# Linear attention and a convolved feed-forward block: query factors sent through memory, kv by heads, one PSUM store

## The chip, the cores and the metric

The kernel runs on one core of a Trainium2 chip. The engines are named as in the profile: PE is TensorE (its weight loads are listed as PEld), DVE is VectorE, ACT is ScalarE, POOL is GpSimd, and SP issues the DMAs. The metric is the device time of one execution in microseconds. A shorter time is better.

## What is computed

Four batches of four heads, 1088 positions, 32 columns a head. All arrays are float32 to the kernel; S1, S2 and the feed-forward weights arrive as float64 and are turned into float32 on the chip.

```
def phi(x):                       # r = 8
    a = einsum('rd,bhsd->bhsr', S1, x)
    b = einsum('rd,bhsd->bhsr', S2, x)
    return einsum('bhsi,bhsj->bhsij', a, b)   # 64 features per head
kv  = einsum('bhsf,bhsd->bhfd', phi(k), v)
z   = sum over s of phi(k)
x   = (phi(q) @ kv) / (phi(q) @ z + 1e-6)     # heads side by side: 128 columns
h   = max(x @ w_in, 0)                        # 128 -> 1024
c   = conv over the sequence, 3 taps, per feature
out = (h * sigmoid(c)) @ w_out                # 1024 -> 128
```

## The kernel before

The sequence of a batch is cut into 9 chunks of 128 positions, taken in 3 groups of 3 (`GC`, `NG`). The kernel has four parts.

*Keys, per batch and group.* `k_ab` (L518) projects a chunk by S1 and S2 at once; ACT copies the result out of PSUM (`k_take`, L522); `k_phi` forms the outer products with `outer` (L502) on DVE or POOL, as the table `kphi` says; `k_kv` (L556) multiplies them with v on two PE tiles of 128x64, each for two heads, so half of each result belongs to the wrong head and `k_kvmask` (L567) clears it. `k_kvt` transposes it and `k_kvtake` (L575) copies it. `k_z` (L536) multiplies the two key factors on one 32-column tile, `k_zmask` and `k_wz` (L544) turn that into 32 further columns of the query weights `wq`, so that the denominator comes out of the query projection.

*Queries, per batch and group.* `q_ab` (L583) projects, `q_take` (L587) copies, `q_ac`, `q_sum`, `q_rec`, `q_div` (L591 to L604) make the denominator and divide the first factor by it, `q_phi` forms the outer product (table `qphi`), `q_t` (L618) transposes it in six 128x128 pieces, `q_ttake` (L622) copies them, `q_x` (L628) multiplies by kv on two 128x64 tiles. `q_hi` (L642) and `q_lo` (L645) split x into two parts for the feed-forward products.

*Feed-forward.* The columns of all batches stand in one row and are cut into 9 segments of up to 510 columns (`SEGS`), times 8 blocks of features: 72 units. A unit runs `f_in` (three matmuls, L673 to L675), `f_relu` and `f_mid` on ACT (L680, L684), two taps on DVE (L688), `f_gate` on ACT (L694), `f_mul` on POOL (L699; the last unit on DVE) and `f_out` (L704), which accumulates over the 8 feature blocks. `f_store` (L710, L715) copies a segment and stores it.

*Weights.* `to_f32` (L428 to L465) converts the float64 words in pieces, with five passes on DVE, two on ACT and one on POOL.

The order of the work is planned in the program itself: `graph` lists each step with a cost and a key, `schedule` places them on four engines by those costs, and `in_order` (L731) issues them in that order, which then holds on each engine. Loads are issued first, in the order of the string `loads`, all from SP. Until 22 us of the plan, gaps on PE are filled with warming matmuls (L414). PSUM has eight banks: four for feed-forward units (`u`), one for the accumulation (`o`), three for everything else (`t`). All inputs have SBUF space of their own.

Of the kernel before, what the change touches and what calls it, by code (L numbers as in the profile page):

```python
# [31 lines left out]

GC = 3
NG = NCH // GC
GT = GC * P
NT = [min(GT, S - g * GT) for g in range(NG)]

# [9 lines left out]
C_ID = 0  # L47
C_KM = C_ID + P
C_ZM = C_KM + P
C_END = C_ZM + HR  # L50

W_S = 2 * HR
T_S2 = 0
T_CW = T_S2 + P
T_END = T_CW + NF * KT

# [3 lines left out]
LOADED = 512  # L60

CFG = {
    "loads": "s t k0 c v0 i0 q0 o0 o1 k1 i1 v2 k3 v1 q2 k2 v3 q1 q3",

    "F0": 16775.11,
    "P": 1995.06,
    "wlead": 1515.06,  # L70
    "outlag": 5.22,
    "tapa": 1050.8,
    "tkey": -31343.46,

    "kdue": [-105657.0, -48463.0, 35025.0, 47292.0],
    "kstep": [9195.0, 4315.0, -973.0, 12517.0],
    "kvlag": -871.37,

    "qlead": [[91584.0, 16163.0, 35465.0], [13701.0, 19977.0, 21211.0], [30185.0, 23965.0, 16558.0], [30572.0, 32036.0, 9517.0]],

    "kphi": ["DPP", "PPP", "PPP", "DPD"],
    "qphi": ["DPP", "DDD", "PPP", "PPP"],

    "late": 1,
    "fills": 22000.0,
}

POOLS = {"u": 4, "o": 1, "t": 3, "h": 6, "s": 3, "g": 6, "f": 3, "w": 3, "kab": 6, "kp": 4, "qs": 3, "qp": 2, "qt": 4, "kv": 2}
BEGIN = {"PE": 1100.0, "ACT": 3000.0, "DVE": 1800.0, "POOL": 1400.0}
KB = {"s": 64, "t": 156, "c": 147, "k": 557, "v": 590, "q": 557, "i": 524, "o": 524}  # L90
SEM = 45.0
FILL = 430.0

def c_pe(occ):
    return "PE", occ, occ + 170 + SEM, False


def c_act(n, ptr=0):  # L100
    return "ACT", 0.833 * n + 52 + 93 * ptr, 0.833 * n + 186 + 93 * ptr + SEM, False
# [10 lines left out]

def graph(cfg):
# [3 lines left out]
    landed = {}  # L117


    def ev(name, cost, deps, alloc=(), uses=(), key=0.0):  # L120
        for b, kind in alloc:
            kind_of[b] = kind
            users[b].append(name)
        for b in uses:
            users[b].append(name)
        events[name] = (cost, deps, [b for b, _ in alloc], key)

    issue, done = 730.0, 0.0
    for name in cfg["loads"].split():
        issue += 420  # L130
        done = max(issue + 1450, done) + KB[name[0]] / 0.345
        landed["dma", name] = done + 250

    for w, n, key in (("s", W_S, -5e4), ("t", T_END, cfg["tkey"])):
# [9 lines left out]
    ev("wqs", c_pool(B * W_S, 1.0), [("s", "value")], key=-4e4)  # L144

    f0, step = cfg["F0"], cfg["P"]
    for w in "io":
        for j in range(NCV):
            d, n = ("dma", f"{w}{j * CVT // LOADED}"), CVT
            key = f0 + (j * CVT // P + (0 if w == "i" else 3.2)) * step - cfg["wlead"]  # L150
            b, bf, bw = ("cv", w, j), ("f", w, j), ("w", w, j)
            ev((w, j, "e"), c_dve(n), [d], [(b, "t")], key=key)
            ev((w, j, "m"), c_dve(n), [d, (w, j, "e")], uses=[b], key=key)
            ev((w, j, "clamp"), c_dve(n), [(w, j, "e")], uses=[b], key=key)
            ev((w, j, "low"), c_act(n), [d], [(bf, "f")], key=key)
            ev((w, j, "f"), c_dve(n), [(w, j, "m"), (w, j, "low")], uses=[b, bf], key=key)
            ev((w, j, "power"), c_act(n), [(w, j, "clamp")], uses=[b], key=key)
            ev((w, j, "sign"), c_dve(n), [(w, j, "power")], [(bw, "w")], [b], key)
# [5 lines left out]
    def unit_of(b, g):  # L164
        c = 1 + b * PITCH + g * GT
        return next(s for s in range(NSEG) if OFF[s] + SEGS[s] + 2 > c) * NF

    def outer(name, where, deps, bank, alloc, uses, key):
        if where == "D":
            ev(name, c_dve(GC * H * RR), deps, [alloc], [bank, *uses], key)  # L170
        else:
            ev(name, c_pool(GC * H * RR, 1.745), deps, [alloc], uses, key)

    for b in range(B):
        due, ks, lag = cfg["kdue"][b], cfg["kstep"][b], cfg["kvlag"]
        for g in range(NG):
            key, t, kp, kv, ab = due + g * ks, ("kps", b, g), ("kp", b, g), ("kvps", b), ("kab", b, g)
            ev(("k_ab", b, g), c_pe(670), [("s", "value"), ("dma", f"k{b}")], [(t, "t")], key=key)
            ev(("k_take", b, g), c_act(192), [("k_ab", b, g)], [(ab, "kab")], [t], key)
            outer(("k_phi", b, g), cfg["kphi"][b][g], [("k_take", b, g)], t, (kp, "kp"), [ab], key)  # L180
            before = [("k_kv", b, g - 1)] if g else []
            ev(
                ("k_kv", b, g),
                c_pe(650),
                [("k_phi", b, g), ("dma", f"v{b}"), *before],
                [] if g else [(kv, "t")],
                [kv, kp] if g else [kp],
                key + lag,
            )
        key = due + 2 * ks  # L190
        abs_ = [("kab", b, g) for g in range(NG)]
        ev(("k_z", b), c_pe(580), [("k_take", b, g) for g in range(NG)], [(("zps", b), "t")], abs_, key)
        ev(("k_zmask", b), c_dve(32), [("k_z", b), ("dma", "c")], uses=[("zps", b)], key=key)
        ev(("k_wz", b), c_pe(270), [("k_zmask", b), ("t", "value")], [(("wzps", b), "t")], key=key)
        ev(("k_wq", b), c_act(32), [("k_wz", b)], uses=[("wzps", b)], key=key)
        key += lag
        ev(("k_kvmask", b), c_dve(128), [("k_kv", b, NG - 1), ("dma", "c")], uses=[("kvps", b)], key=key)
        ev(("k_kvt", b), c_pe(110), [("k_kvmask", b)], [(("kvtps", b), "t")], key=key)
        ev(("k_kvtake", b), c_act(128), [("k_kvt", b)], [(("kv", b), "kv")], [("kvtps", b)], key)
        for g in range(NG):  # L200
            key, q, x, qp = f0 + unit_of(b, g) * step - cfg["qlead"][b][g], ("qps", b, g), ("xps", b, g), ("qp", b, g)
            qs = ("qs", b, g)
            ev(("q_ab", b, g), c_pe(670), [("k_wq", b), "wqs", ("dma", f"q{b}")], [(q, "t")], key=key)
            ev(("q_take", b, g), c_act(192), [("q_ab", b, g)], [(qs, "qs")], [q], key)
            ev(("q_ac", b, g), c_dve(96), [("q_take", b, g)], uses=[q, qs], key=key)
            ev(("q_sum", b, g), c_dve(108), [("q_ac", b, g)], uses=[qs], key=key)
            ev(("q_rec", b, g), c_dve(72), [("q_sum", b, g)], uses=[qs], key=key)
            ev(("q_div", b, g), c_dve(96), [("q_rec", b, g)], uses=[q, qs], key=key)
            outer(("q_phi", b, g), cfg["qphi"][b][g], [("q_div", b, g)], q, (qp, "qp"), [qs], key)
            for pr in range(2):  # L210
                t, qt = ("qtps", b, g, pr), ("qt", b, g, pr)
                ev(("q_t", b, g, pr), c_pe(330), [("q_phi", b, g)], [(t, "t")], [qp], key)
                ev(("q_ttake", b, g, pr), c_act(384), [("q_t", b, g, pr)], [(qt, "qt")], [t], key)
            deps = [("q_ttake", b, g, 0), ("q_ttake", b, g, 1), ("k_kvtake", b)]
            uses = [("qt", b, g, 0), ("qt", b, g, 1), ("kv", b)]
            ev(("q_x", b, g), c_pe(700 * NT[g] / GT), deps, [(x, "t")], uses, key)
            ev(("q_hi", b, g), c_act(NT[g]), [("q_x", b, g)], uses=[x], key=key)
            ev(("q_lo", b, g), c_dve(NT[g]), [("q_hi", b, g)], uses=[x], key=key)

    for u in range(NU):  # L220
        s, f = divmod(u, NF)
        n, key = SEGS[s], f0 + u * step
# [96 lines left out]
def body(ctx: ExitStack, tc: tile.TileContext, qT, kT, v, pk, ps, pt, w_in, w_out, outT):  # L319
# [404 lines left out]
    for u in range(NU):  # L724
        ffn(u)
# [51 lines left out]
```

## Time and profile before

| what | value |
|---|---|
| time, median of 3 runs | 180.09 us (179.15 to 180.49) |
| span of the profiled execution, first to last instruction | 177.1 us |
| instructions | 2740 |
| granted TensorE clock, mean | 0.998 |
| read from memory, written | 9.28 MB, 2.23 MB |

No time of its own is given for the profiled execution beside its span; the median of the runs is 3.0 us above that span.

A group row of the profile names line, engine, operation, output and inputs by the program's names, shapes and count; then the total busy time, the mean of one instruction, and the idle time before it with what ended it. A row of the chain or the timeline begins with its start and its length in us. A row of a table of stretches gives the ends, the length, and the busy time of each engine with the number of instructions in brackets. In the slices of the span each digit is a busy share in tenths.

### The profile page before, as it was taken

The page shows a single profiled execution, that of the slowest core. Times are in us where ns is not written, and L with a number is a line of the kernel's source. Part 1 is how long each engine was busy: PE and PEld are TensorE (multiplying, and loading weights), DVE is VectorE, ACT ScalarE, POOL GpSimd, SP SyncE. Part 2 cuts the span into 40 slices and gives each one's busy share as a digit, 9 for nine tenths or more (in the row PEclk, how much of TensorE's full clock was granted, in tenths as well). Part 3 has the DMA queues.
Part 4 walks back from the last instruction along what each step waited for, and adds up shares of the span by engine and source line. Part 5 has one row for each costly group of instructions (what it writes and reads, how often), then busy time and mean ns, then how long its engine had stood idle before and what let it go on. Part 6 is the DMA issues. An engine that isn't in the chain of part 4 may idle for free.

```text
span 177.1 us, 2740 instructions
## 1 busy us (share of the span) xinstructions
PE 168.1 (95%) x872; PEld 109.2 (62%) x872; DVE 147.1 (83%) x288; ACT 145.6 (82%) x308; POOL 121.2 (68%) x116
## 2 busy tenths in 40 slices
PE   7997789998999999999999999999999999999992
PEld 6875567586766665755675655766455666566630
DVE  5259888969999786968897898899789999989981
ACT  4046558969997987998997989989999999999960
POOL 2065996686986446586766867689558699777670
PEclk9999999999999999999999999999999999999999
DMA  5999991000001000010000001000100100100101
GB/s 163 324 339 422 415 396 43 4 2 0 0 4 44 2 0 0 0 63 0 0 29 34 4 0 59 0 0 0 63 0 0 59 0 2 44 15 4 59 0 47
DMA packets 4477, 11.68 MB, mean 66 GB/s; under 512 B 496, under 2 KB 2416, under 8 KB 4464
## 3 DMA queue, kind: packets, MB, share of 16 engines
q1 hardware_dynamic: 4464, 11.51, 17.6%
q8 instruction: 7, 0.11, 0.3%
q14 instruction: 6, 0.05, 0.1%
HBM read 9.28 MB, written 2.23 MB: 65 GB/s over the span
## 4 chain that ended last, share of the span: by engine, by line
PE 83%; DVE 5%; POOL 4%; ACT 4%; issue 1%; POOLq 1%; ACTq 0%
PE o L704 33%; PE a L673 10%; PE a L674 8%; PE a L675 8%; PE t L556 5%; PE t L628 4%; PE t L618 4%; PE warm L414 4%; PE t L583 3%; POOL kp L502 3%; PE t L518 2%; POOL qp L502 1%; PE t L536 1%; ACT em L454 1%; ACT a L684 1%
## 5 line engine op out<-in xcount | busy, mean ns | idle before, releaser
L688 DVE SCALAR_TENSOR_TENSOR a<-h,pts,a 128x510 f32<-128x510 f32 (+2 forms) x144 | 102.6, 724 | 12.7 <-ACT a L684 9.9
L699 POOL TENSOR_TENSOR g<-h,s 128x510 f32<-128x510 f32 (+2 forms) x71 | 86.4, 1224 | 37.3 <-ACT s L694 30.3
L704 PE MATMUL o<-g,w_out_sb 128*128 128x510 f32 (+2 forms) x144 | 71.0, 579 | 0.4 <-POOL g L699 0.4
L684 ACT ACTIVATE a<-h,pts 128x510 f32<-128x510 f32 (+2 forms) x72 | 49.3, 686 | 0.9
L673 PE MATMUL a<-xhi,whi 128*128 128x512 f32 (+2 forms) x72 | 46.6, 648 | 0.9 <-ACT s L694 0.9
L680 ACT ACTIVATE h<-a 128x512 f32<-128x512 f32 (+2 forms) x72 | 42.2, 587 | 6.1 <-PE a L675 6.0
L694 ACT ACTIVATE s<-a 128x510 f32<-128x510 f32 (+2 forms) x72 | 41.9, 586 | 2.2 <-DVE a L688 1.8
L704 PEld LDWEIGHTS o<-g,w_out_sb 128*128 128x128 f32 x144 | 25.2, 189 | 10.7 <-POOL g L699 4.7
L674 PE MATMUL a<-xhi,wlo 128*128 128x512 f32 (+2 forms) x72 | 27.6, 384 | 0.0
L675 PE MATMUL a<-xlo,whi 128*128 128x512 f32 (+2 forms) x72 | 27.6, 383 | 0.0
L673 PEld LDWEIGHTS a<-xhi,whi 128*128 128x128 f32 x72 | 13.6, 189 | 15.2 <-issue 8.5
L674 PEld LDWEIGHTS a<-xhi,wlo 128*128 128x128 f32 x72 | 13.7, 190 | 9.9 <-issue 9.5
L502 POOL TENSOR_TENSOR kp<-kab 128x768 f32<-128x768 f32 x9 | 13.5, 1514 | 4.8 <-ACT kab L522 4.8
L675 PEld LDWEIGHTS a<-xlo,whi 128*128 128x128 f32 x72 | 13.5, 188 | 2.4
L622 ACT COPY qt<-t 128x384 f32<-128x384 f32 x24 | 11.8, 498 | 0.8 <-PE t L618 0.8
L502 POOL TENSOR_TENSOR qp<-qn,qab 128x768 f32<-128x768 f32 x8 | 12.0, 1514 | 0.4 <-DVE qn L604 0.4
L618 PEld LDWEIGHTS t<-pks,qp 128*128 128x128 f32 x72 | 8.5, 140 | 5.7 <-issue 1.6
L618 PE MATMUL t<-pks,qp 128*128 128x128 f32 x72 | 10.8, 275 | 0.6 <-DVE qd L600 0.3
L556 PE MATMUL t<-kp,vt 128*64 128x128 f32 x144 | 10.5, 281 | 0.7 <-POOL kp L502 0.6
L583 PE MATMUL t<-wq,qt 128*128 128x96 f32 x72 | 10.0, 277 | 1.2 <-issue 0.4
L583 PEld LDWEIGHTS t<-wq,qt 128*128 128x128 f32 x72 | 9.2, 191 | 3.1 <-issue 1.1
L518 PEld LDWEIGHTS t<-sab,kt 128*128 128x128 f32 x72 | 9.2, 191 | 2.9 <-ACT kab L522 1.6
(71 smaller groups left out, 142.9 us busy)
## 6 DMA issues: line engine op xcount, KB each, us to landing
vt<-in_v SPq DMA_DIRECT2D x4, 576.0 KB, 11.9
kt<-in_kT SPq DMA_DIRECT2D x4, 544.0 KB, 10.9
qt<-in_qT SPq DMA_DIRECT2D x4, 544.0 KB, 11.9
w_in_raw<-in_w_in SPq DMA_DIRECT2D x2, 512.0 KB, 9.2
w_out_raw<-in_w_out SPq DMA_DIRECT2D x2, 512.0 KB, 9.6
out<-o SPq DMA_DIRECT2D x4, 255.0 KB, 2.0
out<-o SPq DMA_DIRECT2D x1, 201.5 KB, 1.9
out<-o SPq DMA_DIRECT2D x1, 191.0 KB, 1.9
```

The lines of the kernel that those rows point to most:

```text
L502: e.tensor_tensor(out=out.rearrange("p c (h i j) -> p (c h) i j", i=R, j=R), in0=a.unsqueeze(3).broadcast_to([P, n, R, R]), in1=b.unsqueez ...
L583: nc.tensor.matmul(pv[:, :, j, :], qt[:, b, c * P : (c + 1) * P], wq[:, b], start=True, stop=True)
L618: nc.tensor.transpose(ps[:, j * P : (j + 1) * P], st["qp", g][:, j, P * pr : P * (pr + 1)], ident)
L673: nc.tensor.matmul(a[:, : n + 2], whi[:, w], xhi[:, x], start=True, stop=False)
L674: nc.tensor.matmul(a[:, : n + 2], wlo[:, w], xhi[:, x], start=False, stop=False)
L675: nc.tensor.matmul(a[:, : n + 2], whi[:, w], xlo[:, x], start=False, stop=True)
L680: nc.scalar.activation(h[:, : n + 2], a[:, : n + 2], AF.Relu)
L684: nc.scalar.activation(st["a"][:, :n], h, AF.Copy, scale=cw[:, f, 1:2])
L688: nc.vector.scalar_tensor_tensor(out=a[:, :n], in0=h[:, k : n + k], scalar=cw[:, f, k : k + 1], in1=a[:, :n], op0=ALU.mult, op1=ALU.add)
L694: nc.scalar.activation(s[:, :n], st["a"][:, :n], AF.Sigmoid)
L699: e.tensor_tensor(out=gt[:, :n], in0=st["h"][:, 1 : n + 1], in1=st["s"][:, :n], op=ALU.mult)
L704: nc.tensor.matmul(acc[g][:, :n], w_out_sb[:, f * P : (f + 1) * P], st["g"][:, :n], start=f == 0, stop=f == NF - 1)
```

## The change

*kv.* `k_kv` issues one matmul per chunk and head, 32 columns of v against the 64 features of that head, on four PE tiles of 128x32; the mask is gone. `k_kvtwo` copies the result twice side by side on ACT before the transpose. `k_z` is spread over four tiles of 32 columns; their sum is made by `k_wz`, whose weights are four copies of S2, made and transposed on the chip.

*Queries of batches 1 to 3.* The two factors of a chunk are not multiplied where they are: both halves of the batch (five and four chunks) are laid side by side, transposed in five pieces (`r_t`, `r_take`), written to a tensor in memory in two pieces (`r_put`), and read back by six DMAs (`rep`), the first factor with each row repeated eight times, the second with each block of eight rows repeated eight times. Their product (`q_prod`, on POOL for batches 1 and 2 and on DVE for batch 3) is the transposed outer product. Batch 0 keeps the old way.

*q_x.* For all batches four matmuls, one per head, on PE tiles of 64x32.

*Buffers.* The seven PSUM banks beside the accumulator become one store `p` for all uses. Six SBUF rows (`row`) are used in turn by the loaded k and q of a batch, the raw weights, and the replicated factors.

*Loads and groups.* k and q of batch 0 come in three parts, the weights in eight pieces; the identity is made on POOL instead of loaded. k of batches 1 to 3 is taken in groups of five and four chunks. `kphi` goes from DPP, PPP, PPP, DPD to PDD, DD, PP, PP, and `qphi` from DPP, DDD, PPP, PPP to PDD for batch 0 and P, P, D for the products.

*End.* In the last segment the last two feature blocks are split into halves of 202 columns, with an accumulator and a store for each half; the last two units multiply on DVE.

*Plan.* The costs in `graph` and all keys are new, SP is planned as a fifth engine and its order is issued like that of the others, and a change of PE tile shape is counted.

```
-    "loads": "s t k0 c v0 i0 q0 o0 o1 k1 i1 v2 k3 v1 q2 k2 v3 q1 q3",
+    "loads": "s k0.0 c k0.1 k0.2 v0 t q0.1 q0.2 i0 k1 q0.0 i1 v1 o1 i2 i3 q1 o0 o3 o2 k2 v2 k3 q3 v3 q2",
...
-POOLS = {"u": 4, "o": 1, "t": 3, "h": 6, "s": 3, "g": 6, "f": 3, "w": 3, "kab": 6, "kp": 4, "qs": 3, "qp": 2, "qt": 4, "kv": 2}
+POOLS = {"p": 7, "o": 1, "h": 6, "s": 3, "g": 6, "f": 3, "w": 3, "kab": 4, "kp": 3, "qs": 3, "kv": 2, "tt": 2, "r": 2, "row": 6, "out": 2}
...
         def k_z():
+            nq = P // HR
             for c in range(NCH):
...
+                nc.tensor.matmul(
+                    ps[HR * q : HR * (q + 1), :HR],
+                    ab[:, 1, j, :],
+                    ab[:, 0, j, :],
+                    start=c < nq,
+                    stop=c >= NCH - nq,
+                    tile_position=(0, HR * q),
+                )
...
         def k_kv(g):
+            c0, c1 = KG[b][g]
+            for c in range(c0, c1):
+                for h in range(H):
+                    d = slice(D * h, D * (h + 1))
                     nc.tensor.matmul(
-                        ps[64 * pr : 64 * (pr + 1), :P],
-                        vt[:, b, c, 64 * pr : 64 * (pr + 1)],
-                        st["kp", g][:, j, P * pr : P * (pr + 1)],
+                        ps[d, :RR],
+                        vt[b][:, c, d],
+                        st["kp", g][:, c - c0, RR * h : RR * (h + 1)],
                         start=c == 0,
                         stop=c == NCH - 1,
-                        tile_position=(0, 64 * pr),
+                        tile_position=(0, D * h),
                     )
...
-        def k_kvmask():
+        def k_kvtwo():
+            st["kvm"] = kvm = at.tile([P, 2, RR], F32, tag="kvm", name="kvm")
+            nc.scalar.copy(kvm, st["kvps"][:, :RR].unsqueeze(1).broadcast_to([P, 2, RR]))
...
+        def r_t(i):
+            t = tts[slot["tt", b]]
+            st["rtps", i] = ps = bank(("rtps", b, i), "p", "rtps")
+            for j, c in enumerate(range(4) if i == 0 else range(4, HC)):
+                nc.tensor.transpose(ps[:, j * P : (j + 1) * P], t[:, c].rearrange("p c t r -> p (c t r)"), ident)
+
+        def r_take(i):
+            if i == 0:
+                st["r"] = buffer(("r", b), "r", [P, HT], "r")
+            c = slice(0, 4 * P) if i == 0 else slice(4 * P, HT)
+            nc.scalar.copy(st["r"][:, c], st["rtps", i][:, : c.stop - c.start])
+
+        def r_put(c):
+            if "far" not in st:
+                st["far"] = far.tile([2 * HR, S], F32, tag=f"far{b}", name="far")
+            cols = slice(0, HT) if c == 0 else slice(HT, S)
+            n = cols.stop - cols.start
+            nc.sync.dma_start(st["far"][:, cols], st["r"][64 * c : 64 * (c + 1), :n])
+
+        def rep(pr, what):
+            i = int(what != "a")
+            if ("rep", i) not in st:
+                st["rep", i] = rows(("rep", b, i))[:, :, :S]
+            if what == "a":
+                to = st["rep", 0][:, pr]
+                of = st["far"][16 * pr : 16 * pr + 16].unsqueeze(1).broadcast_to([16, R, S])
+            else:
+                h = int(what[1])
+                row = HR + 16 * pr + R * h
+                to = st["rep", 1][RR * h : RR * (h + 1), pr]
+                of = st["far"][row : row + R].unsqueeze(0).broadcast_to([R, R, S])
+            nc.sync.dma_start(to, of)
+
+        def q_prod(c, pr):
+            cols = slice(0, HT) if c == 0 else slice(HT, S)
+            e = nc.vector if CFG["qphi"][b] == "D" else nc.gpsimd
+            e.tensor_tensor(
+                out=st["rep", 0][:, pr, cols], in0=st["rep", 0][:, pr, cols], in1=st["rep", 1][:, pr, cols], op=ALU.mult
+            )
...
         def q_x(g):
-            for pr in range(2):
-                c = slice(64 * pr, 64 * (pr + 1))
+            x0, x1 = XS[b][g]
+            for h in range(H):
+                r, d = slice(64 * (h % 2), 64 * (h % 2 + 1)), slice(D * h, D * (h + 1))
+                of = st["qt", g, h // 2][r, : x1 - x0] if b == 0 else st["rep", 0][r, h // 2, x0:x1]
                 nc.tensor.matmul(
-                    ps[c, : NT[g]],
-                    st["kv"][:, c],
-                    st["qt", g, pr][:, : NT[g]],
+                    ps[d, : x1 - x0],
+                    st["kv"][r, d],
+                    of,
                     start=True,
                     stop=True,
-                    tile_position=(0, 64 * pr),
+                    tile_position=(64 * (h % 2), D * h),
                 )
...
-            e = nc.vector if u >= NU - CFG["late"] else nc.gpsimd
+            e = nc.vector if u >= len(UNITS) - CFG["late"] else nc.gpsimd
```

More of the change, by code (lines that the diff above doesn't have):

```diff
@@ L125, in ev @@
             users[b].append(name)
[L126 to L134, printed above, removed]
+        events[name] = (cost, list(deps), [b for b, _ in alloc], key)
+    for n, name in enumerate(cfg["loads"].split()):
+        w = place(name)
+        ev(("dma", name), c_dma(load_kb(name)), [], [(w, "row")] if w and w not in kind_of else [], [w] if w in kind_of else [], -1e9 + n)
+    ev(("ident",), c_pool(256, 1.0), [], key=-9e5)
+    for w, n, key in (("s", W_S, -5e5), ("t", T_END, cfg["tkey"])):
         d = ("dma", w)
@@ new lines, in graph @@
+        puts = [("r_put", b, 0), ("r_put", b, 1)]
+        for pr in range(2):
+            key = due - cfg["rlead"] + 1 + pr
+            for what, i, eng in (("a", ra, 16), ("b0", rb, 8), ("b1", rb, 8)):
+                alloc = [(i, "row")] if pr == 0 and what != "b1" else []
+                more = [] if alloc else [("rep", b, 0, "a" if what == "a" else "b0")]
+                ev(("rep", b, pr, what), c_dma(4 * S * (64 if eng == 8 else 128) / 1e3, eng), puts + more, alloc, [] if alloc else [i], key)
@@ L264, in schedule @@
     waiting = collections.defaultdict(list)
+    rank = {name: i for i, name in enumerate(events)}
     slot, begin, fills = {}, {}, {}
-    now, port = dict(BEGIN), {"DVE": 0.0, "POOL": 0.0}
+    now, port, mode, wire = dict(BEGIN), {"DVE": 0.0, "POOL": 0.0}, "128x128", 0.0
     last = 0.0
@@ L279, in finish @@
                 waiting[events[m][0][0]].append(m)
-    for name, t in landed.items():
-        finish(name, t)
+    for name, n in missing.items():
+        if not n:
+            waiting[events[name][0][0]].append(name)
     for _ in range(len(events)):
         best = None
-        for e in ("PE", "ACT", "DVE", "POOL"):
+        for e in ("SP", "PE", "ACT", "DVE", "POOL"):
             able = []
@@ L575, in k_kvtake, with chunks @@
             nc.scalar.copy(kv, st["kvtps"][:, :P])
+        def chunks(g):
+            return range(g * GC, (g + 1) * GC) if b == 0 else range(g * HC, min((g + 1) * HC, NCH))
         def q_ab(g):
-            ps = bank(("qps", b, g), "t", "t")
-            st["qps", g] = pv = ps[:, : 3 * GC * HR].rearrange("p (t c r) -> p t c r", t=3, r=HR)
-            for j in range(GC):
-                c = g * GC + j
-                nc.tensor.matmul(pv[:, :, j, :], qt[:, b, c * P : (c + 1) * P], wq[:, b], start=True, stop=True)
@@ new lines, in q_ab @@
+            for j, c in enumerate(cs):
+                nc.tensor.matmul(pv[:, :, j, :], qt[b][:, c * P : (c + 1) * P], wq[:, b], start=True, stop=True)
+        def q_take(g):
+            if b == 0:
+                st["qab", g] = ab = buffer(("qs", b, g), "qab", [P, 2, GC, HR], "qab")
+                nc.scalar.copy(ab, st["qps", g][:, :2])
+            else:
+                n = len(chunks(g))
+                nc.scalar.copy(tts[slot["tt", b]][:, :n, g].rearrange("p c t r -> p t c r"), st["qps", g][:, :2])
```

600 lines of the change are left out of this document (377 added, 223 removed).

## The prediction

> **What bounds the kernel now.** I read the busy shares first, then the 40 slices, the chain that ended last, a table of four stretches, and the chain in order of time.
>
> ```profile
> PE 168.1 (95%) x872; PEld 109.2 (62%) x872; DVE 147.1 (83%) x288; ACT 145.6 (82%) x308; POOL 121.2 (68%) x116
> ...
> PE   7997789998999999999999999999999999999992
> ...
> GB/s 163 324 339 422 415 396 43 4 2 0 0 4 44 2 0 0 0 63 0 0 29 34 4 0 59 0 0 0 63 0 0 59 0 2 44 15 4 59 0 47
> ...
> PE 83%; DVE 5%; POOL 4%; ACT 4%; issue 1%; POOLq 1%; ACTq 0%
> ```
>
> PE is busy in every slice but the last and owns 83% of the chain; the input DMA ends after six slices of 4.43 us. The four stretches are the start, the first feed-forward units, the long middle and the tail:
>
> ```profile
> 0.00:23.00 23.00, 19.32 (x141) 15.51 (x141) 14.99 (x54) 9.52 (x27) 11.63 (x25) 1.00 0.91 335
> 23.00:30.00 7.00, 6.38 (x73) 5.09 (x72) 5.80 (x15) 5.45 (x14) 5.45 (x7) 1.00 0.57 227
> 30.00:170.00 140.00, 139.14 (x656) 87.70 (x655) 123.73 (x217) 129.51 (x265) 102.36 (x85) 1.00 0.04 15
> 170.00:177.10 7.10, 3.25 (x8) 0.89 (x6) 2.55 (x5) 1.08 (x3) 1.72 (x2) 0.95 0.08 29
> ```
>
> After the length stand PE, PEld, DVE, ACT, POOL, the granted clock, the DMA share and GB/s. From 30 to 170 us PE stands at 139.1 of 140 with the clock at 1.00, so what is taken off PE there comes off the time, until ACT (129.5) takes over. Busy spans overlap and flatter PE, so I take its prices from the chain in order of time, where each piece runs to the start of the next:
>
> ```profile
> 72.56 0.66 PE t L618 x6
> ...
> 76.30 0.80 PE t L628 x4
> 77.09 0.42 PE a L673
> ...
> 80.38 0.81 PE t L556 x12
> ...
> 82.09 0.85 PE o L704 x2
> 82.94 0.23 PE a L673
> ...
> 83.65 0.85 PE o L704 x2
> ...
> 92.02 0.69 PE t L536 x18
> ```
>
> A matmul on plain float32 is two records. L704 streams 510 columns in 0.85 us: 1.67 ns a column. L556 is six matmuls of 128 columns: one after another they would take 6 x 128 x 1.67 = 1.28 us; it took 0.81, so its two 128x64 column tiles ran side by side (0.64) with 0.17 us of entry. L628 says the same: two times 384 columns in 0.80, not 1.28. Behind it L673 takes 0.42 instead of 0.23, so leaving such tiles costs 0.19. A full unit repeats on PE every 83.65 - 82.09 = 1.56 us. ACT is nearly as full; one unit's three passes, back to back, repeat after 135.70 - 134.14 = 1.56 us too:
>
> ```profile
> 134.14 0.71 ACT L684 ACTIVATE a<-h,pts 128x510 f32<-128x510 f32 x1
> 134.75 0.61 ACT L680 ACTIVATE h<-a 128x512 f32<-128x512 f32 x1
> 135.22 0.62 ACT L694 ACTIVATE s<-a 128x510 f32<-128x510 f32 x1
> 135.70 0.73 ACT L684 ACTIVATE a<-h,pts 128x510 f32<-128x510 f32 x1
> ```
>
> **The change part by part.** The sum is made against the profiled span, 177.1 us. The median of the runs, 180.1, lies 3.0 above it; those 3.0 us are carried over unchanged.
>
> (a) The q transposes. Twenty-four groups of three (L618: 0.66 for two, 0.33 each) become six, for batch 0, and 15 transposes of factors at 0.11 for the others: -18 x 0.33 + 15 x 0.11 = **-4.3 us** on PE.
>
> (b) kv by heads: four tiles of 32 columns, 64 columns streamed, for two tiles and 128. If four run abreast, nine chunks stream 9 x 64 x 1.67 = 0.96 us, with two or three entries of 0.17 some 1.4, against 3 x 0.81 = 2.43 now: 1.0 off a batch. If its 72 short records flow only at the rate of L536 (18 in 0.69, 38 ns each) they take 2.76, 0.3 more a batch. Ends -4.0 and +1.3; I take **-4.0**, because L556 is the same operation and shows tiles abreast, while L536 sits on a single tile.
>
> (c) k_z over four tiles: 0.69 falls to 0.36 at best. Ends 0 and -1.3; I take **-1.0**. The kv groups fall from 12 to 9, three exits fewer: 3 x 0.19 = **-0.6**. The turn of S2 and the new k_wz are single small matmuls, nothing.
>
> (d) q_x on four 64x32 tiles. Each head streams n columns; four abreast take 1.67 n, as the two tiles do now: **0**. Two abreast would add 0.64 per 384 columns, over 4352 columns 7.3 us. No gain is possible, since each head's columns must stream. I take 0 of the ends 0 and +7.3, as the column tiles above all ran abreast.
>
> A page speaks against this part. The Trainium skill, TensorEngine Tiling (Array Packing), Gotcha 1: PSUM Pressure, says that different row tiles cannot access one PSUM bank at the same time; heads 0 and 1 lie in different row halves and write one bank. By that rule the sum ends 7.3 us higher. No row tile is in this trace, so nothing here bears on it yet.
>
> (e) ACT, POOL and DVE.
>
> ```profile
> L622 ACT COPY qt<-t 128x384 f32<-128x384 f32 x24 | 11.8, 498 | 0.8 <-PE t L618 0.8
> L699 POOL TENSOR_TENSOR g<-h,s 128x510 f32<-128x510 f32 x56 | 71.2, 1279 | 32.5 <-ACT s L694 25.7 <-PE t L518 1.9 <-PE o L704 1.7
> L699 POOL TENSOR_TENSOR g<-h,s 128x404 f32<-128x404 f32 x7 | 7.2, 1040 | 1.7 <-ACT s L694 1.5
> L502 POOL TENSOR_TENSOR qp<-qn,qab 128x768 f32<-128x768 f32 x8 | 12.0, 1514 | 0.4 <-DVE qn L604 0.4
> ```
>
> ACT loses 18 copies of 0.50 (9.0) and gains three pairs of factor copies, about 0.6 and 0.3 by their sizes (2.7), and four kv copies of about 0.3 that DVE's mask did before (1.1): -5.2. A product column on POOL costs (1279 - 1040) / 106 = 2.25 ns, so the 2176 columns of a batch make 4.9 and, with four starts, some 5.4 us against 3 x 1.51 = 4.5 now; POOL is free for 37 of the 140 middle us and hides it. On DVE the larger outer products of kv and the dropped ones of q about cancel: 0. What PE gives up runs into ACT, though: it had 10.5 us free in the middle stretch; with 9.9 off PE and 5.2 off ACT about 6 of 130 stay. Engines that full wait for each other: I add **+2.0**, between 0 (all still fits) and +5 (half of PE's gain goes).
>
> (f) The way through memory. A batch sends 0.28 MB out and reads 2.23 MB back: at the 396 to 422 GB/s of the late loads 6.2 us, and two landings of about 1.9 make 10.
>
> ```profile
> out<-o SPq DMA_DIRECT2D x4, 255.0 KB, 2.0
> ...
> 61.25 0.48 PE L673 MATMUL a<-xhi,whi 128*128 128x512 f32 x1
> ```
>
> The second row is the 17th unit, the first that reads batch 1. It would now come near 54. Batch 1's q is moved ahead in the load order, to some 4.8 MB, which by the rates above land by 16 us; projection and division follow by 20 or so. SP issues in order, so its eight DMAs stand behind the last loads (to about 27 us): back by 37, multiplied by 43. That leaves 11 us of cover. I cost it at **0**; behind a late product on POOL would stand the feed-forward products, for which PE's second matmul waits. The output stores stand behind the same DMAs on SP; they land in 2 us and nobody waits for them before the end.
>
> (g) The start.
>
> ```profile
> L414 PE MATMUL warm<-idle 128*128 128x256 f32 x20 | 7.1, 523 | 1.1 <-POOL idle L397 1.1
> 1.65 0.42 SPq L370 DMA_DIRECT2D kt<-in_kT  x1
> DMA to landing us min/median/max: 4.0/10.9/12.6
> 3.70 0.22 DVE L465 TENSOR_TENSOR sab<-e,f 128x64 f32<-128x64 f32 x1
> 7.38 2.12 PE L518 MATMUL t<-sab,kt 128*128 128x64 f32 x18
> 9.27 2.98 POOL L502 TENSOR_TENSOR kp<-kab 128x768 f32<-128x768 f32 x2 [4.80 <-ACT kab L522]
> 23.04 0.42 PE L673 MATMUL a<-xhi,whi 128*128 128x384 f32 x1
> 26.35 0.88 PE L556 MATMUL t<-kp,vt 128*64 128x128 f32 x12 [0.62 <-POOL kp L502]
> ```
>
> Of the first 23 us PE did real work in 19.3 - 7.1 = 12.2. Batch 0's k landed near 6 (1.65 + 4.0, plus its issue), and 18 warming matmuls kept PE until 7.4. Its first third now follows 0.25 MB of bytes and needs no later start than the weights at 3.9: about 3 us earlier. Two of three outer products then run beside POOL's on DVE, not two on POOL in a row (2.98). The q third that the first unit needs is loaded late, behind some 2.6 MB, about 10.2 us, no earlier than now; so the first unit moves only from 23.0 to about 19. Ends: -1 (q and weights hold it) and -6 (the whole 3 plus the POOL wait at 26.35 and the second product). I take **-4.0**.
>
> (h) The tail.
>
> ```profile
> 167.94 0.34 PE L675 MATMUL a<-xlo,whi 128*128 128x406 f32 x1
> 171.52 0.51 ACT L694 ACTIVATE s<-a 128x404 f32<-128x404 f32 x1 [0.81 <-DVE a L688]
> 172.06 0.58 DVE L699 TENSOR_TENSOR g<-h,s 128x404 f32<-128x404 f32 x1 [0.63 <-ACT s L694]
> 173.68 0.58 DVE L710 COPY o<-o 128x404 f32<-128x404 f32 x1 [1.04 <-PE o L704]
> ```
>
> From the last hidden matmul to the end of the span is 9 us, passes over 404 columns one after another. Halves of 202 save, by 0.51 / 404 and 0.58 / 404, at most 0.25 each on three ACT and four DVE passes, and 0.34 on the last matmul: 2.1 at most, less the starts that do not shrink (about 0.7), plus one POOL product of 1.04 that goes to DVE. I take **-2.2**, ends -1 and -3.
>
> Sum: -4.3 - 4.0 - 1.0 - 0.6 + 0 + 2.0 + 0 - 4.0 - 2.2 = -14.1; span 163.0, time **166.0 us**.
>
> **The rivals.** *q_x two abreast* (d). For it: four narrow tiles in both halves of the rows are new here. Against: column tiles overlapped in both lines that use them. Time 166.0 + 7.3 = 173.3.
>
> *The gain is half eaten.* ACT and DVE (123.7 of 140) are so full that PE's gain turns into waits for them, or the records of (b) stay at 38 ns. For it: the full ACT row above. Against: POOL's slack and the idle of ACT. With +5 for +2.0 in (e) and +1.3 for -4.0 in (b): 174.3.
>
> *Slower: the way through memory is late.* POOL waits in order for the replicated rows, the feed-forward products queue behind it, then PE. Price: each batch's overrun, three times. The 14.1 us are gone when each batch overruns by 4.7, and the time passes 181.9 at 5.3 each. Batch 1 has 11 us of cover, so its round trip must take 26 us rather than 10; less the two landings that is 2.5 MB in 22 us, 113 GB/s, about a quarter of what the loads reached. With 20 us lost over the three batches the time is 186. For it: the trace has no copy of one row to eight partitions. Against: idle DMA from 27 us on.
>
> The Trainium skill, DMA: Bandwidth & Descriptors, Rules for kernel authors, says that a transfer whose outermost dimension is a broadcast of c copies uses at most c engines. Four of a batch's six reads have eight copies outermost. By it their 1.11 MB take twice as long, some 2.7 us more in the round trip, still under the cover. No such transfer is in this trace.
>
> *Better.* Every part at its good end (start -6, k_z -1.3, tail -3, no give-back): 160.9.
>
> **How the numbers follow.** Forecast 162 to 169.5: 0.53. Better, under 162: 0.12. q_x two abreast: 0.11. Half eaten: 0.11. No change, where the last two meet: 0.04. Slower: 0.09. About 1% is what a measurement of this kernel can tell from no change, since its three runs spread over 0.7%. So faster 0.87, within 1% 0.04, slower 0.09. The range 159.5 to 175.5 leaves out the slower case, the no-change case and the outer ends of better and half eaten, 0.2 in all.
>
> **What would show it.** Right: transposes of the factors at 0.11 each; the kv groups at about 0.5 us for three chunks; q_x at about 0.8 for 384 columns; first feed-forward unit near 19 us; POOL's products never the last before a feed-forward product; the time after the last hidden matmul near 7 us. Wrong: q_x at 1.3, kv at 0.9, DVE or ACT as the releaser of PE through the middle, or a stretch in which POOL stands idle for a DMA of the replicated rows.

## The result, and the profile after

The changed kernel takes 164.39 us (median of 4 runs, 162.27 to 165.61) against 180.29 (179.15 to 181.32) for the kernel before in the same session: a ratio of 0.9055, 95% interval 0.8978 to 0.9133. Ratios here and below leave out disturbed runs, those more than 1.5% above the fastest of their kernel. The profiled run took 162.27 us with a span of 160.3, which is 16.8 less than the span before; the 2.0 us outside the span stand where the prediction carried 3.0.

First the page of the changed kernel: busy shares, three rows of the slices, the shares of the chain that ended last.

```profile
PE 151.9 (95%) x1036; PEld 102.1 (64%) x1036; DVE 142.0 (89%) x283; ACT 137.6 (86%) x301; POOL 121.6 (76%) x119
...
PE   7988999899999999699999999999999999999992
...
PEclk9999999999999999999999999999999999999999
...
GB/s 93 255 385 389 404 403 319 90 164 201 179 119 179 228 226 171 183 201 86 0 0 69 0 0 53 16 0 0 65 0 0 58 10 2 0 69 0 2 65 52
...
PE 45%; ACT 20%; DVE 13%; DMA 11%; SPq 4%; issue 3%; POOL 2%; DVEq 0%; POOLq 0%; ACTq 0%
```

PE is still busy 95% of the span, but it owns 45% of the chain where it owned 83%. ACT, DVE and DMA have come in. The row of GB/s has a second hump, slices 8 to 19, at about half the rate of the first: the replicated rows. One PE slice, the 17th, falls to 6.

The stretches of the changed kernel: the start behind the warming, five microseconds of it with loads alone on the DMA, the middle, the tail.

```profile
5.00:30.00 25.00, 23.11 (x356) 19.44 (x356) 21.29 (x69) 15.87 (x50) 14.34 (x13) 1.00 0.92 341
...
18.00:23.00 5.00, 5.00 (x75) 4.01 (x71) 4.77 (x16) 4.01 (x14) 3.27 (x4) 1.00 1.04 408
30.00:155.00 125.00, 122.83 (x664) 77.91 (x664) 116.91 (x196) 119.51 (x248) 104.54 (x87) 1.00 0.27 77
155.00:160.30 5.30, 2.16 (x12) 1.68 (x11) 2.02 (x6) 0.48 (x2) 0.81 (x2) 0.94 0.12 39
```

The middle lost 15 us of length and kept PE full: 122.8 of 125, where it was 139.1 of 140. So PE's work went, as the prediction meant it to. What went is read in the chain in order of time:

```profile
38.78 0.70 PE kvps L714 x40
39.48 0.69 PE rtps L807 x5
40.17 0.58 PE kvps L714 x32
...
51.94 12.95 DMA rows<-far
65.05 1.54 POOL rows L839
66.64 1.27 PE xps L849 x12
...
75.01 0.94 PE xps L849 x8
...
101.74 1.21 PE xps L849 x16
```

All of a batch's kv is 0.70 + 0.58 = 1.28 us, for 2.43 before. Five transposes of factors take 0.69, of which 0.19 is the exit from the narrow tiles ahead of them: 0.10 each. q_x takes 0.94 for 448 columns and 0.60 for 320 (two groups in 1.21). And there is a piece that the kernel before had nothing like: 12.95 us of DMA for replicated rows, then POOL's product, then q_x. That is where the weak slice lies.

The timeline of the changed kernel, a few rows of PE, SP and POOL (the bracket is the idle time ahead and what ended it):

```profile
1.17 3.78 PE L550 MATMUL warm<-idle 128*128 128x256 f32 x8 [1.17 <-POOL idle L528]
4.74 1.38 PE L664 MATMUL kps<-sab,rows 128*128 128x64 f32 x6
26.82 0.43 PE L891 MATMUL a<-xhi,whi 128*128 128x384 f32 x1
27.79 0.38 PE L686 MATMUL zps<-kab 128*32 128x32 f32 x18 [0.20 <-ACT kab L669]
28.10 1.10 PE L664 MATMUL kps<-sab,rows 128*128 128x64 f32 x8
...
28.25 1.53 SPq L820 DMA_DIRECT2D far<-r  x2
...
44.16 2.66 POOL L839 TENSOR_TENSOR rows<-rows 128x640 f32<-128x640 f32 x2
65.05 1.53 POOL L839 TENSOR_TENSOR rows<-rows 128x640 f32<-128x640 f32 x1 [2.04 <-DMA rows<-far]
66.64 1.27 PE L849 MATMUL xps<-rows,kv 64*32 64x320 f32 x12 [1.47 <-POOL rows L839]
68.17 0.39 PE L892 MATMUL a<-xhi,wlo 128*128 128x512 f32 x1
...
152.71 0.27 PE L893 MATMUL a<-xlo,whi 128*128 128x204 f32 x1
```

The wait for the rows passes from POOL (2.04) to PE (1.47). The real work begins at 4.74 instead of 7.38, yet the first feed-forward unit starts at 26.82, later than the 23.04 before. Eighteen products of k_z take 28.10 - 27.79 = 0.31 for 0.69. From the last hidden matmul, at 152.71, 7.6 us are left to the end of the span, for 9.2.

### The profile page after: what moved, and what is told of

Same layout as the page of the kernel before. It is cut to its first block, busy times and chain, and to the rows that moved or that the text cites. A ratio compares the mean times of both kernels' runs of the same rounds, so it can differ in the third digit from the quotient of the medians.

```text
span 160.3 us, 3125 instructions
## 1 busy us (share of the span) xinstructions
PE 151.9 (95%) x1036; PEld 102.1 (64%) x1036; DVE 142.0 (89%) x283; ACT 137.6 (86%) x301; POOL 121.6 (76%) x119
## 4 chain that ended last, share of the span: by engine, by line
PE 45%; ACT 20%; DVE 13%; DMA 11%; SPq 4%; issue 3%; POOL 2%; DVEq 0%; POOLq 0%; ACTq 0%
PE o L926 21%; DMA rows<-far 8%; ACT s L912 7%; PE a L891 6%; PE a L892 6%; PE a L893 6%; ACT a L902 6%; ACT h L898 4%; DMA rows<-in_w_in 3%; PE xps L849 3%; DVE f L579 2%; DVE em L576 2%; DVE kp L648 2%; DVE em L573 2%; DVE em L570 2%
## 5 line engine op out<-in xcount | busy, mean ns | idle before, releaser
L906 DVE SCALAR_TENSOR_TENSOR a<-h,cwt,a 128x510 f32<-128x510 f32 (+3 forms) x148 | 100.1, 708 | 5.4 <-ACT a L902 3.1
L917 POOL TENSOR_TENSOR g<-h,s 128x510 f32<-128x510 f32 (+3 forms) x72 | 86.5, 1217 | 17.4 <-ACT s L912 14.1
L902 ACT ACTIVATE a<-h,cwt 128x510 f32<-128x510 f32 (+3 forms) x74 | 53.3, 740 | 0.3
L891 PE MATMUL a<-xhi,whi 128*128 128x512 f32 (+3 forms) x74 | 51.0, 689 | 0.3 <-ACT s L912 0.3
L912 ACT ACTIVATE s<-a 128x510 f32<-128x510 f32 (+3 forms) x74 | 46.0, 641 | 1.0 <-DVE a L906 0.7
L898 ACT ACTIVATE h<-a 128x512 f32<-128x512 f32 (+3 forms) x74 | 44.9, 644 | 1.1 <-PE a L893 1.0
L892 PE MATMUL a<-xhi,wlo 128*128 128x512 f32 (+3 forms) x74 | 28.1, 380 | 0.0
L893 PE MATMUL a<-xlo,whi 128*128 128x512 f32 (+3 forms) x74 | 28.0, 378 | 0.0
L839 POOL TENSOR_TENSOR rows<-rows 128x640 f32<-128x640 f32 (+1 forms) x8 | 10.7, 1345 | 3.0 <-DMA rows<-far 2.0
L648 POOL TENSOR_TENSOR kp<-kab 128x1024 f32<-128x1024 f32 (+2 forms) x5 | 10.2, 2046 | 1.8 <-ACT kab L669 1.8
```

Source lines behind the costliest of these rows:

```text
L648: e.tensor_tensor(out=out.rearrange("p c (h i j) -> p (c h) i j", i=R, j=R), in0=a.unsqueeze(3).broadcast_to([P, n, R, R]), in1=b.unsqueez ...
L891: nc.tensor.matmul(a[:, : n + 2], whi[:, w], xhi[:, x], start=True, stop=False)
L892: nc.tensor.matmul(a[:, : n + 2], wlo[:, w], xhi[:, x], start=False, stop=False)
L893: nc.tensor.matmul(a[:, : n + 2], whi[:, w], xlo[:, x], start=False, stop=True)
L898: nc.scalar.activation(h[:, : n + 2], a[:, : n + 2], AF.Relu)
L902: nc.scalar.activation(st["a"][:, :n], h, AF.Copy, scale=cw[:, f, 1:2])
```

## The experiments

Four questions were open: do the narrow tiles run abreast and is that where the time went (a1, a2, b1); does the way through memory cost anything, and why (b2, d1, b4, b6); what are the halves at the end worth (b3); what bounds the kernel now, and what holds the start (c1, b5). The kernels ran in three groups, each beside the kernel before; the changed kernel was run again in the second and the third.

**a1: the kernel before, with kv by heads alone.** The mask on DVE stays and reads the narrower result.

```
-                for pr in range(2):
+                for h in range(H):
+                    d = slice(D * h, D * (h + 1))
                     nc.tensor.matmul(
+                        ps[d, :RR], vt[:, b, c, d], st["kp", g][:, j, RR * h : RR * (h + 1)], ...
+                        tile_position=(0, D * h),
```

> The kernel before with one part of the change: kv by heads on four 128x32 tiles, everything else and the order of issue as before. If PE is the bound and four tiles run abreast, a group of three chunks falls from 0.81 us to about 0.47, 12 groups give 4 us: about 176 us. If its short records flow only at 38 ns each, it is 181 us or more. If the gain of the whole change comes from the new plan and not from PE work, it stays at 180 us.

Measured 176.32 us (176.09 to 176.36) against 179.3; ratio 0.9821 (0.9782 to 0.9859). The chain of a1:

```profile
49.45 0.47 PE t L557 x24
49.92 0.84 PE o L710 x2
```

Three chunks in 0.47 us, for 0.81, of which 3 x 64 x 1.67 ns = 0.32 is streaming. The four tiles ran abreast, and their short records did not flow at L536's pace. Twelve such groups save 12 x 0.34 = 4.1 of PE; the time gave back 3.0 (179.3 - 176.3). Three of the twelve are batch 0's, at the start, where PE also waits for other things (up to 0.60 for POOL's outer products); the other nine make 9 x 0.34 = 3.1, which fits.

**a2: the kernel before, with q_x on four 64x32 tiles alone.**

```
-            for pr in range(2):
+            for h in range(H):
+                r, d = slice(64 * (h % 2), 64 * (h % 2 + 1)), slice(D * h, D * (h + 1))
                 nc.tensor.matmul(
+                    ps[d, : NT[g]], st["kv"][r, d], st["qt", g, h // 2][r, : NT[g]], ...
+                    tile_position=(64 * (h % 2), D * h),
```

> The kernel before with q_x on four 64x32 tiles, all else as before. If the four heads run abreast although two row halves write one PSUM bank, a group of 384 columns stays near 0.80 us and the time at 180 us. If row halves cannot share a bank, a group takes about 1.4 us and the time is about 187 us.

Measured 179.62 us (10 runs, 178.55 to 182.96); ratio 0.9986 (0.9955 to 1.0016). The chain of a2:

```profile
54.53 0.78 PE t L628 x8
55.31 1.05 PE o L704 x2
```

Four tiles, 384 columns: 0.78, where two took 0.80. The Trainium skill, TensorEngine Tiling (Array Packing), Gotcha 1: PSUM Pressure, says that different row tiles cannot access one PSUM bank at the same time. By that rule it would have been about 1.4, and the time 7.3 us longer. The trace does not agree: heads 0 and 1 sit in different row halves and wrote one bank here, on different partitions, and still ran side by side.

**b1: the changed kernel, with kv on two tiles again** (all else kept but the copy behind it, which takes the 128 columns as they are).

```
-                for h in range(H):
-                    d = slice(D * h, D * (h + 1))
+                for pr in range(2):
+                    d = slice(64 * pr, 64 * (pr + 1))
```

> The changed kernel with kv back on two 128x64 tiles over 128 columns, its order of issue unchanged. If PE work sets the time of the changed kernel as well, it loses four times 2.43 less 1.28, that is 4.6 us: about 169 us. If ACT or the way through memory has become the bound, PE has slack and it loses less than 2 us.

Measured 166.08 us (164.88 to 166.5); ratio 0.9238 (0.9179 to 0.9298), with 0.9055 for the changed kernel in an earlier session. The profiled span is 164.1, 3.8 above 160.3. The chain of b1:

```profile
17.65 1.24 PE kvps L714 x20
...
20.01 1.02 PE kvps L714 x16
```

A batch's kv is 2.26 there for 1.28: four batches make 3.9 us of PE, and the spans of the two profiles differ by 3.8. The medians, of different sessions, differ by 1.7, within the changed kernel's own spread of 3.3. The ratios differ by 1.8%, with intervals apart, but the unchanged kernel moved as far between two sessions (0.9261 in `after_again` below). So b1 shows the PE work come back; of the time it shows only that it agrees.

**b2: the second factor's reads without replication.** Each fetches 64 stored rows, each once, in place of eight rows eight times.

```
-                of = st["far"][row : row + R].unsqueeze(0).broadcast_to([R, R, S])
+                of = st["far"][0 : RR]
```

> The changed kernel where the second factor's reads fetch 64 different rows of the stored factors (the wrong ones) in place of eight rows repeated eight times: same bytes, same number of DMAs. If the eight outermost copies hold these reads to half of the DMA engines, the rate between 31 and 65 us rises from some 180 to over 250 GB/s, the stall of 1.5 us in front of the second batch's q_x goes, and the time is 1 to 2 us lower, about 163 us. If the reads are slow for another reason, rate and time stay.

**d1: all replicated rows read from k's input instead.** As many bytes; each DMA reads its 64 or 128 rows once, and none of them is written by the kernel. The six DMAs of a batch read the same rows of k again.

```
-                of = st["far"][16 * pr : 16 * pr + 16].unsqueeze(1).broadcast_to([16, R, S])
+                of = kT[b]
...
-                of = st["far"][row : row + R].unsqueeze(0).broadcast_to([R, R, S])
+                of = kT[b][0:RR]
```

> The changed kernel where the 18 reads of replicated factors fetch rows of k (each once, the wrong data) and so wait for no store: same bytes and DMAs. If the reads are slow because few rows are read again and again, the rate in the stretch from 31 to 65 us goes from some 180 to over 300 GB/s, the wait of POOL for rows goes, and the time falls by 1 to 2 us. If the reads are slow for a cause at the receiving side or in the DMA engines, the rate stays near 240 GB/s.

The same 11 us of each, in the table of stretches (DMA share and GB/s stand last). The changed kernel:

```profile
54.00:65.00 11.00, 11.00 (x43) 5.81 (x42) 10.04 (x16) 10.87 (x22) 7.36 (x6) 1.00 0.81 194
```

b2, and the row of PE's timeline that ends a stall:

```profile
54.00:65.00 11.00, 11.00 (x54) 6.00 (x48) 10.08 (x16) 10.94 (x23) 10.20 (x9) 1.00 1.03 240
```

```profile
45.98 0.34 PE L893 MATMUL a<-xlo,whi 128*128 128x384 f32 x1 [2.80 <-issue]
```

d1, and the same:

```profile
54.00:65.00 11.00, 11.00 (x55) 5.93 (x54) 10.25 (x18) 10.94 (x23) 10.28 (x9) 1.00 1.03 296
```

```profile
37.26 2.53 PE L743 MATMUL qps<-wq,rows 128*128 128x96 f32 x17 [3.17 <-issue]
```

In these 11 us two things change, one behind the other. The eight-copy reads leave some of the engines idle: without them a share of 0.81 becomes 1.03, and 194 GB/s become 240. The Trainium skill, DMA: Bandwidth & Descriptors, Rules for kernel authors, states that an outermost broadcast of c copies confines a DMA to at most c engines. The trace agrees in direction. But with all engines busy b2 still came at 240, d1 at 296, and the loads of the start at 408. So most of the way from 408 to 194 is not the eight outermost copies. What the rest is stays open: b2 still repeats each row of the first factor eight times, and d1 changes that, the source and the wait for the stores at once.

Over the whole stretch that the two expectations name, neither rise came. From 31 to 44 us the rates are 170 (changed kernel), 194 (b2) and 180 GB/s (d1), from 44 to 54 us 174, 95 and 81, and so from 31 to 65 us 179, 179 and 188. The low rates of b2 and d1 in the middle stand behind a stall of PE, the rows shown above, behind which the next transfers on SP come later (d1's next store at 45.28 for 40.71, b2's next read at 50.02 for 47.81). Such a mean does not tell how fast the engines can go, and 54 to 65 us is one stretch of one run each.

The times settle less. b2 took 163.74 us (162.56 to 166.33), ratio 0.91 (0.9038 to 0.9162), no different from the changed kernel. d1 took 165.36 (161.11 to 166.81), and no ratio can be given. In both, the wait for late rows is gone, and in its place PE stood still once, for 2.80 and 3.17 us, waiting for nothing that the profile shows, with the DMA engines full just ahead of it (b2: a share of 1.01 from 40 to 43 us) or all through it (d1: 1.02 from 34.0 to 37.2). Full engines are not needed for it: b3, below, has the same stall, 2.83 us, at the same instruction of the order as b2, with a share of 0.62 in the 3 us ahead of it.

**after_again: the changed kernel once more**, beside d1, b3 and b4.

> The changed kernel as it is, as the measure for the others of this group: 164 us.

Measured 167.55 us (165.54 to 168.04); ratio 0.9261 (0.9199 to 0.9323), outside the interval of the first session. Its profile, span 165.3, shows what differs. POOL's product of batch 2 and PE behind it:

```profile
64.60 1.53 POOL L839 TENSOR_TENSOR rows<-rows 128x640 f32<-128x640 f32 x1 [5.54 <-DMA rows<-far]
67.41 1.19 PE L926 MATMUL o<-g,w_out_sb 128*128 128x510 f32 x2 [4.28 <-POOL g L917]
68.82 0.63 PE L892 MATMUL a<-xhi,wlo 128*128 128x512 f32 x1
```

and the stretch behind that stall, with the row of the granted clock in 40 slices:

```profile
67.00:73.00 6.00, 5.59 (x24) 2.59 (x25) 2.36 (x4) 3.40 (x7) 4.54 (x5) 0.72 0.51 139
...
PEclk9999999789999999789999999999999999999999
```

POOL stands 5.54 us for the rows, the gated features queue behind it, PE stands 4.28. Then the granted clock is 0.72 over 6 us (a hidden matmul of 512 columns takes 0.63, for 0.39 at full clock), which is 0.28 x 6 = 1.7 us more. Less the 1.47 that PE already stood for the rows in the first profile, this makes 4.28 + 1.7 - 1.47 = 4.5 of the 5.0 us by which the spans differ. The clock row shows an earlier fall too, in slices 8 and 9: the clock was at 0.50 from 30.8 to 34.2 us, with no idle time of PE over 0.5 us in the 6 us ahead, and PE then runs 1.0 us behind the first profile (its transposes of factors start at 40.52 for 39.48). With that the parts make 5.5, half a microsecond more than the difference. The late rows are the "slower" rival of the prediction, small: one batch of three overran.

**b3: no halves at the end** (`SPLIT = 0`), and **b4: the queries of batches 1 to 3 kept on the chip** as in batch 0, so nothing goes through memory.

> The changed kernel without the halved units at the end (the last segment keeps two accumulators and two stores, its last two units are whole). If halves shorten the chain behind the last hidden matmul by (h)'s 2 us less what the stores keep, it is 1.5 us slower, about 166 us. If ACT is the bound at the end and the halves only add starts to it, the time stays.

> The changed kernel with batches 1 to 3 on the old way of q: outer products on DVE (batch 1) and POOL, 18 more groups of transposes and their copies, nothing sent to memory; the order is planned anew from the same keys. If PE and ACT work set the time, 4.1 us of PE come back and some 1.5 us of late rows go: about 167 us. If the way through memory costs as much in waits as it saves on PE, it is 164 us or less.

b3 measured 169.73 us (167.42 to 175.28), ratio 0.9318 (0.9279 to 0.9357) against 0.9261 in the same group: 0.6%, about 1 us, and the intervals overlap. b4 measured 173.78, one run at 168.68 and three from 173.25 to 174.4. The fastest is 0.6 above the slowest run of the changed kernel in this group. The profiled one, 173.25, lost some 6.7 us to a clock of 0.52 from 8 to 22 us and would else lie among them. So what the query part is worth is not shown by a run, neither its size nor, strictly, its sign; the new order of work also makes b4 a poor measure.

**b5: k of batch 0 in one load** instead of three.

```
+                if w == "k":
+                    if g:
+                        return
+                    c = slice(0, S)
```

> The changed kernel with k of batch 0 loaded in one transfer at the place of its first third, the order of issue otherwise unchanged. If the earlier first third is what the start gained (step g), the first projection moves from 4.7 to about 6 us and the time by +1 to +1.5 us. If PE at the start waits for other things (v, the weights, DVE), the time stays within 0.5 us.

**b6: the changed kernel, planned anew with the cost of the rows' reads 1.8 times as high.** The same instructions in another order.

```
-    c_dma(4 * S * (64 if eng == 8 else 128) / 1e3, eng)
+    c_dma(1.8 * 4 * S * (64 if eng == 8 else 128) / 1e3, eng)
```

> The changed kernel planned anew with the reads of replicated rows priced 1.8 times as long, nearer to the rate that the traces show; products and q_x of batches 2 and 3 come later in the order. If late rows in front of an order that waits for them cost the changed kernel 1.5 us in one group and some 5 us in another, POOL waits for rows under 0.5 us here and the time falls by 1 to 4 us against the control. If the new order loses elsewhere what it gains, it is no faster.

**c1: the third hidden matmul left out from unit 24 on.**

```
-            nc.tensor.matmul(a[:, : n + 2], whi[:, w], xlo[:, x], start=False, stop=True)
+            if u < 24:
+                nc.tensor.matmul(a[:, : n + 2], whi[:, w], xlo[:, x], start=False, stop=True)
```

> The changed kernel without the third hidden matmul from unit 24 on (a small correction term of the hidden layer is left out), 50 units of 0.23 us less on PE. If PE alone sets the time of the long stretch, it falls by 9 to 11 us to about 154. If ACT, at 1.56 us a unit, is as full as PE, the unit still repeats every 1.56 us where nothing of attention is left, and the time falls by no more than PE's attention work that then finds room, under 3 us.

**after_control: the changed kernel beside these three.**

> The changed kernel as it is, as the measure for the others of this group: between 164 and 168 us, where the two groups before put it.

The control measured 164.62 us (6 runs, 162.16 to 169.9), ratio 0.9081 (0.9025 to 0.9138).

b5 measured 167.32 (163.88 to 170.39), ratio 0.914 (0.9097 to 0.9184). The first projection starts at 5.19 for 4.74, not at 6, and the first kv product at 9.90 for 8.78. Its two fastest runs, 163.88 and 164.56, lie about 1 us above the control's three fastest, 162.16 to 163.74. The intervals overlap; 1 us is what the rows allow, not what is shown.

b6 measured 162.16 us (4 runs, 161.7 to 162.46), ratio 0.9031 (0.8999 to 0.9063). The middle of b6:

```profile
30.00:155.00 125.00, 124.17 (x668) 78.33 (x668) 116.11 (x196) 119.26 (x248) 105.08 (x88) 1.00 0.30 77
```

PE is idle 0.8 us of the 125, for 2.2; POOL has no wait for rows. In all three profiles of the changed kernel PE stands behind late rows, for 1.47, 4.28 and 2.60 us (the control: 1.39 and 1.21). By the ratios b6 is hardly faster than the control (the intervals overlap), but all four runs lie within 0.8 us, where the control's six spread over 7.7 and five of them lie above b6's slowest. With four runs that is a hint, not a proof, that the late rows made part of the spread. They did not make all of it: the control's run of 169.9 us lost most of its time to the clock, as shown below. b6 is the best version here: below both kernels, by median.

c1 measured 163.44 (162.14 to 168.07), ratio 0.9073 (0.902 to 0.9125): the same as the control, with 0.23 us a unit off PE. Its stretch from 128 us on, and one ACT pass, unit after unit:

```profile
128.00:150.00 22.00, 19.62 (x62) 11.04 (x62) 21.19 (x32) 22.00 (x45) 17.54 (x15) 1.00 0.07 24
134.25 0.81 ACT L899 ACTIVATE h<-a 128x512 f32<-128x512 f32 x1
...
135.82 0.83 ACT L899 ACTIVATE h<-a 128x512 f32<-128x512 f32 x1
```

ACT is busy all 22 us and a unit still takes 135.82 - 134.25 = 1.57, as it did with all three matmuls (1.56 on PE before). The chain of the changed kernel had said so already, with ACT's passes from 129 us on:

```profile
131.05 0.58 ACT a L902
...
132.63 0.58 ACT a L902
...
134.21 0.58 ACT a L902
```

So with the attention done, PE and ACT are full together, and to take work from PE alone gains nothing there. ACT's slack was small earlier too: in c1's chain PE's units come 1.31 us apart at first (80.19 to 81.50), and from 91 us on ACT's passes stand in it. That work taken from ACT alone would gain nothing either was not run; it is what PE's own 1.56 us a unit implies.

The control's profile holds one thing more. It fell on a run of 169.9 us (span 167.9), and its clock went down at the start. The row of the granted clock, the stretch, and the matmul that follows the longest idle time ahead of it:

```profile
PEclk9955589978999999999999999999999999999999
```

```profile
8.00:22.00 14.00, 13.08 (x149) 12.05 (x147) 8.56 (x31) 4.49 (x15) 4.39 (x4) 0.51 1.02 383
```

```profile
9.01 1.51 PE L714 MATMUL kvps<-kp,vt 128*32 128x64 f32 x48 [0.92 <-DMA vt<-in_v]
```

Fourteen us at a clock of 0.51 do the work of about seven: that is nearly the whole difference to 160.3. In the first profile the same matmul waited 0.56 for its load of v and the clock stayed at 1.00; b4's profile has the fall at the same place after a wait of 0.68 (0.52 from 8 to 22 us). The wait alone does not decide it: in d1 this matmul waited 1.33 and the clock stayed at 1.00. The changed kernel warms PE with 8 matmuls, the kernel before with 20, of which 18 stand ahead of its first projection at 7.38; its profile shows no such fall, nor do those of a1 and a2. Whether more warming would prevent it no run tests.

## Why the prediction was right, and where it was not

The prediction said 166.0 us and a span of 163.0; the median is 164.4 and the profiled span 160.3. What it rested on, that PE is the bound and that work off PE comes off the time, is shown by a1 for one part (that part alone: its ratio excludes 1) and agrees with b1 (the part undone). c1 shows where it ends: behind the attention, ACT is as full. One of its signs of being wrong did come, POOL idle for the replicated rows (2.04 us), and one of its signs of being right did not, a first unit near 19 us. By its own steps, against the profiled span:

- **(a) The q transposes, -4.3.** Right in the price: 0.10 each, 15 of them. What it brought in time has no run of its own, since b4 does not settle it.
- **(b) kv by heads, -4.0, and three exits fewer, -0.6.** Right. 2.43 - 1.28 makes -4.6 over four batches without the exits; the bad end, records of 38 ns, is excluded by a1: 24 matmuls in 0.47.
- **(c) k_z, -1.0.** 0.31 where 0.36 was called the best: -1.5, beyond the good end of -1.3.
- **(d) q_x, 0.** Right, by a2 and by the rows of the changed kernel. The rival *two abreast* is out.
- **(e) The give-back, +2.0.** The size was near, the place wrong. PE's idle time in the middle rose from 0.9 to 2.2 us, +1.3, but 1.47 of it is the one wait for late rows of (f). ACT did not slow PE through the middle; it takes over the chain at 129 us, and c1 shows that little more was to be had there from PE alone.
- **(f) The way through memory, 0.** The step that failed. It took the rate of the loads, 396 to 422 GB/s; the rows came at 194 in the stretch shown. It also worked out the cover of batch 1 alone. There the puts started at 28.25, where about 27 had been said, the first product at 44.16 for 43, and the cover held. For batch 2, whose cover was not worked out, it did not hold: 1.5 us in the best profile, 6 in after_again with its lowered clock. The rule of the Trainium skill, DMA: Bandwidth & Descriptors, Rules for kernel authors, would by the prediction's estimate have added 2.7 us to the round trip and still have left it covered, so it was too small as well.
- **(g) The start, -4.0.** Right in size by luck, wrong in mechanism. The first unit came not at 19 but at 26.8. What fell is the time in which PE did no work that counts: before, in the first 30 us, 30 - (19.32 + 6.38) + 7.1 of warming = 11.4; after, 1.17 ahead of the warming, 3.78 of it, and 25 - 23.11 = 1.89, together 6.8. So -4.6, because PE is filled ahead of the first unit with work of later batches whose loads had landed: the projections and kv of batch 1 and the key projection of batch 2. How much of it the earlier loads, the new order and the smaller parts bring is not separated; b5 tests one load, and leaves 1 us open. What counts at the start is the idle time in it, not the time to the first unit.
- **(h) The tail, -2.2.** -1.6: 7.6 us from the last hidden matmul for 9.2. b3's difference of about 1 us agrees with that and does not prove it.

These rows add to -4.3 - 4.6 - 0.6 - 1.5 + 0 + 1.3 - 4.6 - 1.6 = -15.9 of the 16.8; 0.9 has no row of its own. That the time came out nearer to the forecast than the span did, 1.6 off for 2.7, is luck: the median run of the changed kernel lies 2.1 us above its profiled one, and 1.0 less stands outside the span than was carried over. The slower runs of that session have no trace. In the later groups late rows (f) and a lowered clock made runs slower, and neither stood in the sum.

Left open: how much the new order of issue brings by itself, which no run separates from the parts; why b4's runs fall into two groups; what lowers the clock after short idle times; what stopped PE for 2.8 to 3.2 us in b2, d1 and b3; and why the rows come at 240 and 296 GB/s with all engines busy.

## What to carry to other kernels

Where one engine is full over a long stretch and its clock is steady, price an edit by that engine's rows, and believe the sum for that stretch; then ask which engine comes level, for the next edit on the first one may be worth nothing, as in c1. Do not price a transfer of another pattern by the rate of the loads: replicated reads ran here at half of it, and an in-order engine that waits for them passes the delay on to the bound. A plan whose cost for that transfer is too low left waits for rows of 1.5 to 4.3 us in the profiles of this kernel; with a cost 1.8 times as high they were gone, and four runs lay within 0.8 us, which is a hint and not a proof that they had made the spread.

## What the runs showed of the hardware

- PE's granted clock fell to half after stalls of 4.28 us (0.72 over the 6 us behind it) and 3.17 us (d1: 0.50 from 39 to 42 us), and not after 2.80 us (b2: 1.00). It also fell without a long stall: for 14 us at the start in the control and b4, after waits of 0.92 and 0.68 us (0.51 and 0.52), but not in d1 after 1.33; and from 30.8 to 34.2 us in after_again (0.50). The half clock of the Trainium skill, TensorE: Matmul & The Clock Gate, Part 1, agrees in its ratio. A fall after so short a wait had not been expected.
- Four 64x32 tiles in both halves of the rows wrote different partitions of one PSUM bank side by side: 384 columns in 0.78 us, where two 128x64 tiles took 0.80.
- In one stretch of each run, rows read back with eight copies came at 194 GB/s (engine share 0.81), with the second factor's copies left out at 240 (1.03), rows of k at 296 (1.03), the loads of the start at 408 (1.04).
- PE stood for about 3 us with no releaser in the profile in three runs: 2.80 (b2) and 3.17 (d1), with the DMA engines full ahead of it or during it, and 2.83 (b3), at a share of 0.62.
